# Key and value layers of a channel-mix block computed by Strassen's seven block products over 768 tokens

## The chip, the cores and the metric

The kernel runs on one core of one Trainium2 chip. The metric is the device time of one execution in microseconds (us); it is given as the median of several runs. TensorE (PE) does the matmuls, VectorE (DVE), ScalarE (ACT) and GpSimd (POOL) the element work, SyncE (SP) issues most transfers.

## The reference

Attention over 4 batches, 8 heads, 576 positions of 64 features (a coarse part over means of 4 positions plus a local band), then a normalised two-layer block with a residual (512 to 2048 to 512), then the channel-mix block that is changed here:

```python
xk = mu_k * x + (1.0 - mu_k) * x_prev      # x_prev: the token before
xr = mu_r * x + (1.0 - mu_r) * x_prev
k = np.maximum(xk @ w_k, 0.0)              # 512 -> 1024
v = k * k @ w_v                            # 1024 -> 512
r = 1.0 / (1.0 + np.exp(-(xr @ w_r)))      # 512 -> 512
return (r * v).astype(np.float32)
```

## The kernel before

Features lie on the 128 partitions, tokens on the free axis; the 2304 tokens are six chunks of N = 384. Every product of two float32 matrices is made from three matmuls in the reduced format fp32r (mm3, L203): high part times high part, high times low, low times high. For that each operand is split into a rounded copy (ACT) and the rest (DVE subtraction).

The first stage (the loop over c, to about 525 us) computes attention for chunk c + 1 beside the two-layer block of chunk c. slot(c) is called between groups of 12 matmuls, 56 times in each chunk, and lets one step of side work be issued each time: attention, the decoding of the next weights (the inputs are 64-bit floats, read as integers and converted by two ACT and two DVE operations of 128x512, decode, L75), and from chunk 1 on pre_b (L167), which loads, decodes and stores the weights of the last block to DRAM (bd), one step every third slot. In chunk 5, start_b and load_b bring these weights back and split them; emit_x2 writes the block's result x2d to DRAM, four 128x384 rows a chunk: DVE multiplies, POOL adds, POOL issues the stores. Attention's sums over four positions (sums, L241) are chains of adding transfers that POOL issues, each waiting for the one before.

The second stage (the loop over c from L827 on) goes through the six chunks: 8 groups of 12 matmuls for the key layer, 4 groups of 12 for the receptance and 4 groups of 24 for the value layer, 240 matmuls of 384 columns. Key results are evicted by ACT (relu), squared by DVE and split (ACT, DVE) into k2; the receptance takes a DVE clamp, ACT exp, a DVE addition and a DVE reciprocal; a value result is multiplied on DVE into ot and stored. mix(c, which) prepares xk and xr of the next chunk in the background. Matmul results lie in the eight banks of PSUM, used in turn (bank, L814).

The order of instructions on an engine is made by a scheduler that moves an instruction ahead where its inputs are ready sooner; in_order pins an instruction behind what stands before it on its engine, behind does the same for a named pair. Each engine runs its own queue strictly in order.

## Time and profile before

| | before |
|---|---|
| median of 3 runs | 780.17 us (779.93 to 780.19) |
| span of the profiled execution, first to last instruction | 778.9 us |
| PE busy | 761.7 us, 98% |
| DVE, ACT, POOL busy | 516.8, 372.5, 113.6 us |

The profile lists one execution, with its span; the runs' times lie around it, 1.0 to 1.3 us above. Busy time is the time in which an engine had an instruction; a busy PE can still be made of matmuls with gaps inside, so the rate of matmuls is read from first and last start. In the tables of stages, (x) counts instructions started there and PEclk is the granted TensorE clock as a share of full speed.

### The profile page before, as it was taken

How to read it: one execution, taken by the hardware profiler on the slowest of the kernel's cores; microseconds unless marked ns; L12 is line 12 of the kernel's file. 1: busy time of each engine (PE TensorE's matmuls, PEld its weight loads, DVE VectorE, ACT ScalarE, POOL GpSimd, SP SyncE). 2: the span in 40 equal slices, each digit the busy share in tenths (PEclk: the TensorE clock that was granted, in tenths of full speed). 3: DMA queues.
4: the chain of work that ended last, by engine and by line, in shares of the span. 5: the costliest groups of instructions: out<-in, count | busy, mean ns of one | idle time of the engine just before them, and what ended most of it. 6: DMA issues, size and time to landing. Idle time of an engine off the chain costs nothing.

```text
span 778.9 us, 13826 instructions
## 1 busy us (share of the span) xinstructions
PE 761.7 (98%) x5474; PEld 738.4 (95%) x5474; DVE 516.8 (66%) x1018; ACT 372.5 (48%) x840; POOL 113.6 (15%) x148
## 2 busy tenths in 40 slices
PE   5899999999999999999999999999999999999998
PEld 4789898999999999999999999999999999999998
DVE  6879996866456556655664447428949595968664
ACT  4679986455344543554353336317344344535230
POOL 3333300410044404410300030002000000000000
PEclk9859999999999999999999999999999999999999
DMA  8998744344327642744142014302110102010101
GB/s 246 265 295 225 205 140 143 99 116 147 107 79 165 145 131 68 183 123 129 58 124 82 1 42 149 123 1 82 32 50 21 62 11 72 1 42 0 42 1 41
DMA packets 47393, 78.81 MB, mean 101 GB/s; under 512 B 5856, under 2 KB 32096, under 8 KB 47328
## 3 DMA queue, kind: packets, MB, share of 16 engines
q1 hardware_dynamic: 37152, 67.89, 28.0%
q0 software_dynamic: 10176, 10.04, 6.9%
q8 instruction: 43, 0.70, 0.4%
q14 instruction: 22, 0.18, 0.1%
HBM read 63.22 MB, written 14.68 MB: 100 GB/s over the span
## 4 chain that ended last, share of the span: by engine, by line
PE 84%; DVE 7%; ACT 5%; DMA 2%; issue 1%; SPq 0%; ACTq 0%; DVEq 0%
PE b_ps L205 11%; PE b_ps L204 11%; PE b_ps L206 11%; PE acc L204 8%; PE h_ps L204 8%; PE acc L205 7%; PE acc L206 7%; PE h_ps L206 7%; PE h_ps L205 7%; PE av L429 2%; DMA raw<-in_w 2%; PE sc L351 1%; PE scd L347 1%; DVE rm L85 1%; ACT rm L84 1%; ACT rm L80 1%
## 5 line engine op out<-in xcount | busy, mean ns | idle before, releaser
L625 DVE SCALAR_TENSOR_TENSOR hl<-h_ps,hh 128x384 fp32r<-128x384 f32 x96 | 53.1, 553 | 81.9 <-ACT hh L624 81.5
L624 ACT ACTIVATE hh<-h_ps 128x384 fp32r<-128x384 f32 x96 | 46.7, 486 | 97.5 <-PE h_ps L206 97.3
L645 POOL TENSOR_TENSOR x<-x2t,x 128x384 f32<-128x384 f32 x24 | 24.2, 1023 | 302.2 <-DVE x2t L644 302.0
L206 PE MATMUL b_ps<-k,wbl 128*128 128x384 f32 x192 | 64.1, 334 | 0.0
L204 PE MATMUL b_ps<-xk,wbh 128*128 128x384 f32 x192 | 64.1, 334 | 0.0
L205 PE MATMUL b_ps<-xk,wbh 128*128 128x384 f32 x192 | 64.1, 334 | 0.0
L206 PE MATMUL b_ps<-xk,wbl 128*128 128x384 f32 x192 | 64.1, 334 | 0.0
L204 PE MATMUL b_ps<-k,wbh 128*128 128x384 f32 x192 | 64.1, 334 | 0.0
L205 PE MATMUL b_ps<-k,wbh 128*128 128x384 f32 x192 | 64.1, 334 | 0.0
L855 DVE RECIPROCAL e<-e 128x384 f32<-128x384 f32 x24 | 61.0, 2544 | 0.1
L85 DVE SCALAR_TENSOR_TENSOR rm<-rm 128x512 uint32<-128x512 uint32 x52 | 35.6, 688 | 16.3 <-ACT rm L84 15.6
L772 ACT ACTIVATE mixa<-x2in,vec_t 128x384 f32<-128x384 f32 x48 | 28.4, 613 | 37.0 <-DVE xr L775 34.8
L404 ACT COPY PT<-T 32x192 f32<-32x192 f32 x96 | 33.5, 349 | 24.7 <-DVE T L400 23.6
L835 ACT ACTIVATE kr<-b_ps 128x384 f32<-128x384 f32 x48 | 23.5, 490 | 45.5 <-PE b_ps L206 45.4
L247 POOL DMA_DIRECT2D kd<-in_kr x36 | 35.5, 987 | 66.7 <-DMA kd<-in_kr 63.5
L836 DVE TENSOR_TENSOR kr<-kr,b_ps 128x384 f32<-128x384 f32 x48 | 26.5, 552 | 22.6 <-ACT kr L835 22.6
L84 ACT ACTIVATE rm<-raw 128x512 uint8<-128x512 uint8 x52 | 40.3, 785 | 2.2 <-DVE rm L81 1.5
L248 POOL DMA_DIRECT2D vd<-in_vr x36 | 39.3, 1091 | 13.3 <-DMA vd<-in_vr 13.0
L825 DVE TENSOR_TENSOR k<-kr,k 128x384 fp32r<-128x384 f32 x48 | 27.4, 572 | 20.3 <-ACT k L824 20.3
L361 ACT ACTIVATE Pd<-scd,mx 96x144 f32<-96x144 f32 x48 | 17.6, 370 | 40.8 <-DVE mx L358 39.9
L80 ACT ACTIVATE rm<-raw 128x512 f32<-128x512 f32 x52 | 34.4, 669 | 3.8 <-DMA raw<-in_w 3.4
L204 PEld LDWEIGHTS b_ps<-xk,wbh 128*128 128x128 f32 x192 | 36.0, 188 | 0.0
(165 smaller groups left out, 2317.7 us busy)
## 6 DMA issues: line engine op xcount, KB each, us to landing
raw<-in_w SPq DMA_DIRECT2D x32, 512.0 KB, 6.2
v<-in_vw SPq DMA_DIRECT2D x24, 256.0 KB, 3.5
bd<-rm SPq DMA_DIRECT2D x20, 256.0 KB, 2.0
wf<-bd SPq DMA_DIRECT2D x10, 512.0 KB, 4.8
q<-in_qw SPq DMA_DIRECT2D x24, 208.0 KB, 4.1
kz<-in_kw SPq DMA_DIRECT2D x48, 102.0 KB, 2.7
x2d<-x POOLq DMA_DIRECT2D x24, 192.0 KB, 2.2
out<-ot SPq DMA_DIRECT2D x24, 192.0 KB, 1.9
```

The lines of the kernel that those rows point to most:

```text
L80: in_order(pinned, nc.scalar.activation(ru.bitcast(F32), raw.rearrange("p (n t) -> p n t", t=2)[:, :, 1].bitcast(F32), AF.Copy, scale=2.0 ...
L84: in_order(pinned, nc.scalar.activation(low, top, AF.Copy, scale=1.0 / 32.0, bias=-31.0 / 64.0))
L85: in_order(pinned, nc.vector.scalar_tensor_tensor(ru, ru, 3, m, op0=ALU.logical_shift_left, op1=ALU.bitwise_or))
L204: nc.tensor.matmul(ps, wh, ah, start=first, stop=False)
L205: nc.tensor.matmul(ps, wh, al, start=False, stop=False)
L206: nc.tensor.matmul(ps, wl, ah, start=False, stop=last)
L247: in_order(r > 0, eng.dma_start(kd, kr[b, hp, r], **op))
L248: in_order(r > 0, eng.dma_start(vd, vr[b, hp, r], **op))
L404: nc.scalar.copy(PT[p, :, j, :], T[p, :, 0:24])
L624: nc.scalar.activation(hh, ps[:, 0:N], AF.Relu)
L625: last_hl[0] = nc.vector.scalar_tensor_tensor(hl, ps[:, 0:N], 0.0, hh.bitcast(F32), op0=ALU.max, op1=ALU.subtract)
L855: nc.vector.reciprocal(e, e)
```

## The change

The key and value layers are multiplied as 2x2 blocks over two chunks at once (768 tokens, three rounds s instead of six chunks) with seven block products in place of eight (products). Each product is itself the three matmuls of mm3. Sums of weight blocks are formed in the first stage (pre_b: piece and combined), split there and stored to DRAM, and come back ready for use (load_w). Sums of token blocks are formed by seven, on POOL for the key layer and for the value layer of rounds 1 and 2, on DVE for round 0. The last stage is cut in two: all rounds of key and receptance first, with squared keys (kd2) and receptances (rd) stored to DRAM, then all rounds of the value layer, which load them back. The square moves from DVE to POOL, the receptance is one ACT sigmoid. Results in PSUM are read in part before a bank is added to again (after). pre_b takes a step at every slot from chunk 1 to the end of chunk 5.

The diff, cut to its core (the lines that it removes stand in the functions above):

```diff
+    rctx = ExitStack()
+    stg = rctx.enter_context(tc.tile_pool(name="stg", bufs=1, side="right"))
+    xp = rctx.enter_context(tc.tile_pool(name="xp", bufs=2, side="right"))
+    hp_ = rctx.enter_context(tc.tile_pool(name="hring", bufs=HB, side="right"))
...
+    def halves(v, other, dst):
+        store = lambda hl, part: nc.sync.dma_start(dst(hl), part if len(dst(hl).shape) == 2 else part.rearrange("p (k f) -> p k f", k=2))
+        in_order(True, nc.scalar.copy(other.bitcast(F32R), v))
+        yield True
+        store(0, other)
+        in_order(True, nc.vector.tensor_tensor(v.bitcast(F32R), v, other, op=ALU.subtract))
+        yield True
+        store(1, v)
...
+    def piece(src, keep, dst, key=None):
+        t = stg.tile([128, 1024], I32, tag="stg", name="raw", bufs=RB)
+        rm = stg.tile([128, 2, 512], U32, tag="stg", name="rm", bufs=RB)
+        a, b = held(), held()
+        yield from behind_slot(a)
+        nc.sync.dma_start(t if len(src.shape) == 2 else t.rearrange("p (k f) -> p k f", k=2), src)
+        yield True
+        yield True
+        yield from behind_slot(b)
+        g = decode(t, True, rm)
+        w = next(g)
+        other = spare.pop()
+        yield True
+        next(g, None)
+        freed[a] = True
+        yield True
+        if keep is not None:
+            nc.sync.dma_start(keep, w)
+            ready.add(key)
+        if dst is not None:
+            yield from halves(w, other, dst)
+        freed[b] = True
+        yield True
+    def combined(needs, x, y, op, keep, dst, key):
+        t = stg.tile([128, 2, 512], F32, tag="stg", name="comb", bufs=RB)
+        a = held()
+        yield from behind_slot(a)
+        while not needs <= ready:
+            yield False
+        nc.sync.dma_start(t[:, 0], x)
+        nc.sync.dma_start(t[:, 1], y)
+        yield True
+        yield True
+        in_order(True, nc.gpsimd.tensor_tensor(t[:, 0], t[:, 0], t[:, 1], op=op))
+        yield True
+        if keep is not None:
+            nc.sync.dma_start(keep, t[:, 0])
+            ready.add(key)
+        yield from halves(t[:, 0], t[:, 1], dst)
+        freed[a] = True
+        yield True
 
...
+        def quarter(g, m, k):
+            if g < 2:
+                return wks[:, g + 2 * k, 1024 * m:1024 * m + 1024]
+            g -= 2
+            return wvs[:, 4 * k + 2 * g:4 * k + 2 * g + 2, 512 * m:512 * m + 512]
+        def first(g, n):
+            m, k = n // 2, n % 2
+            to = {0: 0, 1: 1, 3: 3}.get(n)
+            return lambda: piece(quarter(g, m, k), fq[:, g, n], None if to is None else (lambda hl: stored(g, to, hl)), ("q", g, n))
+        def second(g, n):
+            A11, A12, A21, A22 = (fq[:, g, i] for i in range(4))
+            x, y, op, keep, to, *needs = {
+                1: (A21, A22, ALU.add, fs[:, g, 0], 4, ("q", g, 2), ("q", g, 3)),
+                2: (fs[:, g, 0], A11, ALU.subtract, fs[:, g, 1], 5, ("s", g, 1), ("q", g, 0)),
+                3: (A11, A21, ALU.subtract, None, 6, ("q", g, 0), ("q", g, 2)),
+                4: (A12, fs[:, g, 1], ALU.subtract, None, 2, ("q", g, 1), ("s", g, 2)),
+            }[n]
+            return lambda: combined(set(needs), x, y, op, keep, lambda hl: stored(g, to, hl), ("s", g, n))
+        jobs = []
+        for g in range(4):
+            jobs += [first(g, 0), first(g, 1)] + ([second(g - 1, 2)] if g else [])
+            jobs += [first(g, 2), first(g, 3)] + ([second(g - 1, 4)] if g else []) + [second(g, 3), second(g, 1)]
+        rest = [(lambda k=k: piece(wrs[:, k, :], None, lambda hl: wrd[:, hl, k, :])) for k in range(4)]
+        jobs += rest[:2] + [second(3, 2)] + rest[2:] + [second(3, 4)]
+        running, todo = [], iter(jobs)
+        while True:
+            while len(running) < RB:
+                j = next(todo, None)
+                if j is None:
+                    break
+                running.append(j())
+            if not running:
+                return
+            for g in list(running):
+                r = next(g, None)
...
@@ emit_x2
-            nc.gpsimd.dma_start(x2d[:, o, N * c:N * c + N], x[:, o, :])
+            st = (nc.gpsimd if c < NCH - 1 else nc.sync).dma_start(x2d[:, o, N * c:N * c + N], x[:, o, :])
+        last_x2.append(st)
...
-        if 1 <= c < NCH - 1 and slots[c] % PRE == 0:
+        if 1 <= c and slots[c] % 3 < PRE:
             next(pre, None)
         if c == NCH - 1 and fd.over():
             if not late:
-                run_all(pre)
                 start_b()
...
+    def load_w(nm):
+        src, W = {"wk": (wkd, WK), "wv": (wvd, WV)}[nm]
+        for p in ORD:
+            W[p] = wpool.tile(list(src.shape[0:1]) + list(src.shape[2:]), F32R, tag="w", name=nm)
+            nc.sync.dma_start(W[p].bitcast(F32), src[:, p])
+            yield
...
+                ld = nc.sync.dma_start(t[:, :, i, 1:SEG + 1], x2d[:, :, n0:n0 + SEG])
+            if s == 1:
+                behind(ld, last_x2[-1])
+        x2in[s] = t
...
+    def mixed(s, which, k, a):
+        t = x2in[s]
+        a4 = a.rearrange("p (i n) -> p i n", i=4)
+        nc.scalar.activation(a4, t[:, k, :, 1:SEG + 1], AF.Copy, scale=vec_t[:, 1 + which, k:k + 1])
+        nc.vector.scalar_tensor_tensor(a4, t[:, k, :, 0:SEG], omu[:, which, k:k + 1], a4, op0=ALU.mult, op1=ALU.add)
+    def seven(B, T, split, eng=nc.gpsimd):
+        sub = lambda o, a, b: eng.tensor_tensor(o, a, b, op=ALU.subtract)
+        B11, B12, B21, B22 = B
+        T1, T2 = T
+        split(0, B11)
+        sub(T1, B12, B11)
+        yield
+        sub(T2, B22, T1)
+        yield
+        split(5, T2)
+        yield
+        sub(B12, B22, B12)
+        split(1, B21)
+        yield
+        split(6, B12)
+        yield
+        sub(T2, B21, T2)
+        split(4, T1)
+        yield
+        split(3, T2)
+        yield
+        split(2, B22)
...
+    def prep_xk(s):
+        ops = xk[s] = {}
+        mt = left[0].tile([128, KT, T2N], F32, tag="mt", name="mt")
+        T = [left[0].tile([128, 2, N], F32, tag=f"T{i}", name="T") for i in range(2)]
+        for k in (0, 2, 1, 3):
+            mixed(s, 0, k, mt[:, k, :])
             yield
+        def split(p, v):
+            t = ops[p] = wpool.tile([128, 2, 2, N], F32R, tag="w", name="xk")
+            nc.scalar.copy(t[:, 0], v)
+            nc.vector.tensor_tensor(t[:, 1], v, t[:, 0].bitcast(F32), op=ALU.subtract)
+        yield from seven([mt[:, 2 * i:2 * i + 2, N * j:N * j + N] for i in range(2) for j in range(2)], T, split)
+    def prep_xr(s):
+        h, l = (right[0].tile([128, KT, T2N], F32R, tag=f"xr{i}", name="xr") for i in range(2))
+        xr[s] = h, l
+        for k in range(KT):
+            a = right[0].tile([128, T2N], F32, tag="mixa", name="mixa", bufs=2)
+            mixed(s, 1, k, a)
+            yield
+            nc.scalar.copy(h[:, k, :], a)
+            nc.vector.tensor_tensor(l[:, k, :], a, h[:, k, :].bitcast(F32), op=ALU.subtract)
             yield
...
-    for g in late["parts"]:
+    for g in [pre] + late["parts"]:
+    rctx.close()
+    right.append(b2ctx.enter_context(tc.tile_pool(name="br", bufs=1, side="right", reuse_waits="tile")))
+    load_x2(1)
...
+    def products(W, X, nk, quarters, done, feed):
+        nq = len(quarters)
+        b = {x: [bank() for _ in range(nq)] for x in "ABE"}
+        p1, u2, u3 = {}, {}, {}
+        def plus(ps, u, nm):
+            t = small(nm)
+            nc.vector.tensor_tensor(t, ps[:, 0:N], u, op=ALU.add)
+            return t
+        def after(p, q):
+            if p == 0:
+                p1[q] = small("p1")
+                nc.scalar.copy(p1[q], b["A"][q][:, 0:N])
+            elif p == 5:
+                u2[q] = plus(b["B"][q], p1[q], "u2")
+            elif p == 1:
+                done(q, 0, 0, b["A"][q], None)
+            elif p == 6:
+                u3[q] = plus(b["B"][q], p1[q], "u3")
+            elif p == 4:
+                done(q, 1, 1, b["E"][q], u3.pop(q))
+            elif p == 3:
+                done(q, 1, 0, b["B"][q], p1.pop(q))
+            else:
+                done(q, 0, 1, b["E"][q], u2.pop(q))
+        for p, x, start in ((0, "A", True), (5, "B", True), (1, "A", False), (6, "B", False), (4, "E", True), (3, "B", False), (2, "E", False)):
+            w = W[p]
+            xh, xl = X[p]
+            for q, cols in enumerate(quarters):
+                ps = b[x][q][:, 0:N]
+                for k in range(nk):
+                    wh, wl = w[:, 0, k, cols], w[:, 1, k, cols]
+                    for i, (a, m) in enumerate(((wh, xh), (wh, xl), (wl, xh))):
+                        nc.tensor.matmul(ps, a, m[:, k, :], start=start and k + i == 0, stop=k == nk - 1 and i == 2, skip_group_check=True)
+                after(p, q)
+                feed()
...
+    def load_wr():
+        for hl in range(2):
+            wr_t.append(wpool.tile([128, KT, 512], F32R, tag="w", name="wr"))
+            behind(nc.sync.dma_start(wr_t[hl].bitcast(F32), wrd[:, hl]), last_x2[-1])
+            yield
+    def rest(n):
+        for _ in range(n):
+            yield
+    bg = [rest(HOLD), load_wr()]
...
+    def prep_v(s, tiles):
+        X = vk[s] = {}
+        Bt, T = tiles()
+        for i in range(2):
+            for j in range(2):
+                n0 = T2N * s + N * j
+                last_kin[:] = [nc.sync.dma_start(Bt[2 * i + j], kd2[:, 4 * i:4 * i + 4, n0:n0 + N])]
+        def split(p, v):
+            h, l = X[p] = [wpool.tile([128, 4, N], F32R, tag="w", name="ko") for _ in range(2)]
+            nc.scalar.copy(h, v)
+            nc.vector.tensor_tensor(l, v, h.bitcast(F32), op=ALU.subtract)
+        yield
+        yield from seven(Bt, T, split, nc.gpsimd if s else nc.vector)
...
+    for s in range(NSC):
+        ops = xk[s]
+        X = {p: (ops[p][:, 0], ops[p][:, 1]) for p in ORD}
+        bg.append(prep_xr(s))
+        if s + 1 < NSC:
+            bg.append(prep_xk(s + 1))
+        else:
+            bg.append(load_w("wv"))
+            bg.append(prep_v(0, from_phase_k))
+        for half in range(2):
+            def done(q, i, j, ps, u):
+                f = 4 * i + 2 * half + q
+                t = small("k", "k", KB)
+                if u is None:
+                    nc.scalar.activation(t, ps[:, 0:N], AF.Relu)
+                else:
+                    nc.vector.tensor_tensor(t, ps[:, 0:N], u, op=ALU.add)
+                    nc.scalar.activation(t, t, AF.Relu)
+                nc.gpsimd.tensor_tensor(t, t, t, op=ALU.mult)
+                n0 = T2N * s + N * j
+                nc.sync.dma_start(kd2[:, f, n0:n0 + N], t)
+            products(WK, X, 2, [slice(128 * (2 * half + q), 128 * (2 * half + q) + 128) for q in range(2)], done, feed)
+        if s + 2 < NSC:
+            load_x2(s + 2)
+        xh, xl = xr[s]
+        for j in range(2):
+            for o in range(KT):
+                ps = bank()
+                c = slice(128 * o, 128 * o + 128)
+                n = slice(N * j, N * j + N)
+                for k in range(KT):
+                    mm3(ps[:, 0:N], wr_t[0][:, k, c], wr_t[1][:, k, c], xh[:, k, n], xl[:, k, n], k == 0, k == KT - 1)
+                t = small("r")
+                nc.scalar.activation(t, ps[:, 0:N], AF.Sigmoid)
+                n0 = T2N * s + N * j
+                nc.sync.dma_start(rd[:, o, n0:n0 + N], t)
+                feed(2)
+        flush()
...
+    for s in range(NSC):
+        if s + 1 < NSC:
+            bg.append(prep_v(s + 1, in_phase_v))
+            feed()
+        def done(q, i, j, ps, u):
+            o = 2 * i + q
+            n0 = T2N * s + N * j
+            r = small("rin", "r", 6)
+            behind(nc.sync.dma_start(r, rd[:, o, n0:n0 + N]), last_kin[0])
+            if u is None:
+                nc.vector.tensor_tensor(r, ps[:, 0:N], r, op=ALU.mult)
+            else:
+                t = small("v")
+                nc.vector.tensor_tensor(t, ps[:, 0:N], u, op=ALU.add)
+                (nc.vector if s == NSC - 1 else nc.gpsimd).tensor_tensor(r, t, r, op=ALU.mult)
+            nc.sync.dma_start(out[128 * o:128 * o + 128, n0:n0 + N], r)
+        products(WV, vk[s], 4, [slice(128 * q, 128 * q + 128) for q in range(2)], done, feed)
+        flush()
+SB = 8
+KB = 5
+HOLD = 6
+NSC = NCH // 2
```

## Rows read from the trace of the kernel before

**Rows 1.** the page's busy time of each engine and the chain that ended last

```profile
...
PE 761.7 (98%) x5474; PEld 738.4 (95%) x5474; DVE 516.8 (66%) x1018; ACT 372.5 (48%) x840; POOL 113.6 (15%) x148
...
PE 84%; DVE 7%; ACT 5%; DMA 2%; issue 1%; SPq 0%; ACTq 0%; DVEq 0%
```

**Rows 2.** busy time by stage: us, busy (x) PE, PEld, DVE, ACT, POOL, PEclk, DMA share, GB/s

```profile
...
608.90:650.50 41.60, 41.60 (x242) 41.60 (x241) 31.34 (x48) 18.04 (x36) 0.00 (x0) 1.00 0.12 39
```

**Rows 3.** the matmuls of the second stage: ns min/median/max, first and last start

```profile
...
L204 PE MATMUL b_ps<-xk,wbh x192: 334/334/334, 525.8 to 749.9; 128*128 128x384 f32 x192
...
L206 PE MATMUL b_ps<-k,wbl x192: 334/334/338, 551.1 to 775.2; 128*128 128x384 f32 x192
```

**Rows 4.** groups by line and shape: out<-in, shapes, xcount | busy us, mean ns

```profile
...
L855 DVE RECIPROCAL e<-e 128x384 f32<-128x384 f32 x24 | 61.0, 2544 | 0.1
...
L772 ACT ACTIVATE mixa<-x2in,vec_t 128x384 f32<-128x384 f32 x48 | 28.4, 613 | 37.0 <-DVE xr L775 34.8 <-DVE xk L775 1.0 <-DMA x2in<-x2d 1.0
L777 DVE SCALAR_TENSOR_TENSOR mixa<-x2in,omu,mixa 128x384 f32<-128x384 f32 x48 | 27.9, 614 | 2.0 <-DMA wf<-bd 1.1 <-ACT mixa L772 0.8
...
L836 DVE TENSOR_TENSOR kr<-kr,b_ps 128x384 f32<-128x384 f32 x48 | 26.5, 552 | 22.6 <-ACT kr L835 22.6
...
L645 POOL TENSOR_TENSOR x<-x2t,x 128x384 f32<-128x384 f32 x24 | 24.2, 1023 | 302.2 <-DVE x2t L644 302.0
L835 ACT ACTIVATE kr<-b_ps 128x384 f32<-128x384 f32 x48 | 23.5, 490 | 45.5 <-PE b_ps L206 45.4
...
L91 DVE TENSOR_TENSOR wbl<-wf,wbh 128x512 fp32r<-128x512 f32 x20 | 12.6, 686 | 6.6 <-ACT wbh L88 6.6
L853 ACT ACTIVATE e<-e 128x384 f32<-128x384 f32 x24 | 12.5, 525 | 29.2 <-DVE e L852 29.2
...
L768 ACT CAST xk<-mixa 128x384 fp32r<-128x384 f32 x24 | 12.1, 508 | 0.0
...
L516 ACT ACTIVATE xc<-xc 128x768 f32<-128x768 f32 x12 | 10.1, 843 | 1.1 <-DVE al L510 1.0
...
L268 POOL TENSOR_TENSOR vr<-vr 72x512 f32<-72x512 f32 x4 | 5.1, 1267 | 25.4 <-DMA vr<-in_vr 25.4
...
L673 ACT ACT_TABLE_LOAD x1 | 1.3, 1283 | 0.7 <-PEq L936 0.7
```

**Rows 5.** one line of attention's norm, six times: ns min/median/max

```profile
...
L518 DVE TENSOR_TENSOR xc<-xc x6: 946/957/2368, 75.9 to 464.2; 128x768 f32<-128x768 f32 x6
```

**Rows 6.** timeline of DVE at three places: start, us, instruction

```profile
...
147.25 2.37 DVE L518 TENSOR_TENSOR xc<-xc 128x768 f32<-128x768 f32 x1
...
461.70 0.56 DVE L644 TENSOR_TENSOR x2t<-acc,y 128x384 f32<-128x384 f32 x1 [1.40 <-POOL x L645]
...
529.72 1.30 DVE L825 TENSOR_TENSOR k<-kr,k 128x384 fp32r<-128x384 f32 x1 [0.58 <-ACT k L824]
```

**Rows 7.** timeline of POOL at the same places

```profile
...
147.76 1.02 POOL L645 TENSOR_TENSOR x<-x2t,x 128x384 f32<-128x384 f32 x1
...
460.65 1.99 POOL L645 TENSOR_TENSOR x<-x2t,x 128x384 f32<-128x384 f32 x2
...
529.56 1.03 POOL L645 TENSOR_TENSOR x<-x2t,x 128x384 f32<-128x384 f32 x1
```

**Rows 8.** busy time by stage, in the first stage

```profile
...
40.00:60.00 20.00, 19.73 (x109) 16.51 (x109) 14.66 (x32) 15.03 (x33) 5.29 (x6) 0.62 0.99 289
...
147.00:525.60 378.60, 378.56 (x2961) 367.50 (x2961) 211.79 (x472) 164.05 (x400) 70.83 (x88) 1.00 0.38 106
...
225.00:302.00 77.00, 77.00 (x633) 74.24 (x632) 45.91 (x105) 36.05 (x89) 25.49 (x31) 1.00 0.53 129
```

**Rows 9.** waits of POOL from 147 to 525 us: total us, times, longest

```profile
...
POOL kd L247 <- DMA kd<-in_kr: 27.1, 15, 3.7
```

**Rows 10.** DMA issues: count, KB each, median us to landing

```profile
...
bd<-rm SPq DMA_DIRECT2D x20, 256.0 KB, 2.0
...
out<-ot SPq DMA_DIRECT2D x24, 192.0 KB, 1.9
```

More of the change, by code (lines that the diff above doesn't have):

```diff
@@ L180, in load_b @@
[L180 to L201 removed]
+    fq = dram.tile([128, 4, 4, 512], F32, name="fq")
@@ new lines, in tile_block, with held, behind_slot @@
+    freed, ready = [], set()
+    def held():
+        freed.append(False)
+        return len(freed) - 1
+    def behind_slot(n):
+        while n >= RB and not freed[n - RB]:
+            yield False
+    def piece(src, keep, dst, key=None):
+        t = stg.tile([128, 1024], I32, tag="stg", name="raw", bufs=RB)
+        rm = stg.tile([128, 2, 512], U32, tag="stg", name="rm", bufs=RB)
+        a, b = held(), held()
[18 more added lines that the diff above has]
+        yield True
@@ L744, in start_b @@
         actx.close()
-        late["bp"] = bp = ctx.enter_context(tc.tile_pool(name="bp", bufs=1))
-        xk.extend(bp.tile([128, KT, NB], F32R, name=f"xk{i}") for i in range(2))
-        late["parts"] = [load_b(), mix(0, 0)]
+        left.append(bctx.enter_context(tc.tile_pool(name="bl", bufs=1)))
+        late["parts"] = [load_w("wk"), prep_xk(0)]
         load_x2(0)
-    def load_x2(c, pinned=False):
-        t = late["bp"].tile([128, KT, 2, SEG + 1], F32, tag="x2in", name="x2in", bufs=2)
-        for i in range(2):
-            n0 = NB * c + SEG * i
+    def load_w(nm):
[4 more added lines that the diff above has]
+            yield
@@ L755, in load_x2 @@
+    def load_x2(s):
+        t = (left if s % 2 == 0 else right)[-1].tile([128, KT, 4, SEG + 1], F32, tag="x2in", name="x2in")
+        for i in range(4):
+            n0 = T2N * s + SEG * i
             if n0 % S:
-                in_order(pinned, nc.sync.dma_start(t[:, :, i, :], x2d[:, :, n0 - 1:n0 + SEG]))
+                ld = nc.sync.dma_start(t[:, :, i, :], x2d[:, :, n0 - 1:n0 + SEG])
             else:
                 nc.gpsimd.memset(t[:, :, i, 0:1], 0.0)
-                in_order(pinned, nc.sync.dma_start(t[:, :, i, 1:SEG + 1], x2d[:, :, n0:n0 + SEG]))
@@ new lines, in small @@
+    def small(nm, tag="s", bufs=None):
+        return (right if tag == "k" else left)[-1].tile([128, N], F32, tag=tag, name=nm, bufs=bufs or SB)
+    def products(W, X, nk, quarters, done, feed):
[33 more added lines that the diff above has]
+                feed()
@@ new lines, in tile_block, with feed @@
+    kd2 = dram.tile([128, NK, B * S], F32, name="kd2")
+    rd = dram.tile([128, KT, B * S], F32, name="rd")
+    wr_t = []
+    def load_wr():
[5 more added lines that the diff above has]
+        for _ in range(n):
+            yield
+    bg = [rest(HOLD), load_wr()]
+    def feed(n=1):
+        for _ in range(n):
+            if bg and next(bg[0], 1) == 1:
+                bg.pop(0)
@@ new lines, in part, with from_phase_k @@
+    def part(t):
+        t = t.rearrange("p a b -> p (a b)") if len(t.shape) == 3 else t.rearrange("p a b c -> p (a b c)")
+        return [t[:, 4 * N * i:4 * N * i + 4 * N].rearrange("p (k n) -> p k n", k=4) for i in range(2)]
+    def from_phase_k():
+        mt = left[0].tile([128, KT, T2N], F32, tag="mt", name="kin")
+        a = right[0].tile([128, KT, 4, SEG + 1], F32, tag="x2in", name="kin")
+        b = left[0].tile([128, KT, 4, SEG + 1], F32, tag="x2in", name="kt")
+        return part(mt) + part(a), part(b)
@@ new lines, in tile_block, with in_phase_v @@
+    b2ctx.close()
+    bctx.close()
+    left.append(ctx.enter_context(tc.tile_pool(name="cl", bufs=1, reuse_waits="tile")))
+    right.append(ctx.enter_context(tc.tile_pool(name="cr", bufs=1, side="right", reuse_waits="tile")))
+    def in_phase_v():
+        T = part(right[-1].tile([128, KT, 4, SEG + 1], F32, tag="x2in", name="kt"))
+        return [right[-1].tile([128, 4, N], F32, tag="kin", name="kin", bufs=4) for _ in range(4)], T
+    for s in range(NSC):
+        if s + 1 < NSC:
+            bg.append(prep_v(s + 1, in_phase_v))
+            feed()
+        def done(q, i, j, ps, u):
[12 more added lines that the diff above has]
+        flush()
```

140 lines of the change are left out of this document (27 added, 113 removed).

## The prediction

> **What bounds the kernel now.** I began with the page: PE is busy 98% of the span, and the chain that ended last is PE for 84%; DVE's 7% and ACT's 5% are small beside it [rows 1]. They come early: from 147 to 525.6 us PE has work in 378.56 of 378.60 us [rows 8]. So where the change acts only two things can change the time: fewer matmuls, or a PE that waits. The stage table says how full the second stage is: in one chunk of 41.6 us PE has no gap, the granted clock is 1.00, and DVE (31.3), ACT (18.0) and POOL (0) have time to spare [rows 2]. First and last start of its matmuls are 525.8 and 775.2 us [rows 3]. A chunk holds 240 matmuls, so one costs 41.6 / 240 = 173.3 ns at 384 columns. That, and not the 334 ns that the rows give a single one (they overlap), is the price that I use. The other views price what the change puts on DVE, ACT and POOL: the groups by shape [rows 4], and a hunt for instructions that lasted longer than others of their line [rows 5 to 7].
>
> **Matmuls: minus 25.0 us.** Per round of two chunks the key layer had 2 x 96 matmuls and the value layer 2 x 96. Now each has 7 products x 8 pairs of 128-blocks x 3 = 168. Three rounds save 3 x 2 x 24 = 144; 144 x 173.3 ns = 25.0 us. Width, type and one weight load per matmul stay, so the price stays. The receptance keeps its 96 a round. What remains is 1296 x 173.3 ns = 224.6 us in place of 249.6.
>
> **Unit prices for the new element work.** DVE on 768 columns: 0.957 us [rows 5]; from 384 (0.552) that is 0.40 more, so the mixing operation of 0.614 becomes 1.02; with 686 ns at 512 columns the slope is 1.05 ns a column, 1.76 us at 1536. ACT: 0.49 to 0.53 at 384, 0.84 at 768, so mixing 0.95 and a split copy of 1536 columns 1.51. POOL: 1.02 at 384 and 1.27 at 512, 1.91 ns a column, so about 1.75 at 768 and 3.2 at 1536 [rows 4]. The sums for 768 and 1536 on POOL and for 1536 on DVE and ACT are estimates on these slopes.
>
> **A rule between DVE and POOL.** A 768-column subtraction or addition took 0.957 us in the median and 2.37 once; that one began at 147.25, and POOL added two SBUF tiles from 147.76 for 1.02. A 384-column split at 529.72 took 1.30 instead of 0.55 while POOL worked from 529.56 for 1.03. But a DVE operation with one input in PSUM ran inside a POOL pair (460.65 to 462.64) in its usual 0.56 [rows 4 to 7]. So a DVE operation on two SBUF tiles is held while POOL adds or multiplies, about as long as the POOL operation lasts. This matters because the change moves squares, block differences and the last products to POOL. The Trainium skill says the like (GPSIMD Engine Reference, Key points: POOL shares its SBUF interfaces with VectorE, in contention with instructions of two SBUF inputs), which the trace bears out; it gives no size. Without such holds the key terms below would be nothing and the time 760.
>
> **Key and receptance stage, per round: 168 + 96 matmuls, 29.1 + 16.6 us.** DVE reads PSUM 20 times (0.552 each, 11.0 us; not held), and does two-tile work of 8 mixings and 11 splits: 8 x 1.02 + 11 x 0.957 = 18.7 us. POOL does 16 squares and 4 differences, 16.4 + 7.0 = 23.4. ACT does 20 evictions, 8 mixings, 11 copies and 8 sigmoids: 31 us. In 45.7 us each fits alone. But 18.7 + 23.4 = 42.1 exclude each other, and most of it is issued in the key part of 29.1.
> PE feels it through the banks. A quarter of a product, six matmuls into one bank, takes 1.04 us, and a round has two halves of 14 quarters. At three products of a half PE adds again into a bank that DVE must have read (after), and comes back to it three quarters (3.1 us) after it was finished. The last such read of a round is the 16th of 20, due 27 quarters = 28.1 us after the start. What DVE must do by then:
> - Round 0: nothing in the background before the new right-hand space is free, when POOL's last row is done at 530.6, 4.8 us after the start [rows 3, 7]; less two reads, 3.7 us idle. Then 16 reads 8.8, four mixings and four splits of xr 7.9, four mixings of xk 4.1, and of ten squares begun by then three quarters in the way (DVE has two-tile work in 12 of 21 us, and a square that meets a read catches the operation behind it) 7.7, one difference 1.3. Sum 33.5: 5.4 us late.
> - Round 1: two xr and four xk mixings are left; the first two xr mixings have buffers of their own and can be done under the receptance. 8.8 + 5.9 + 4.1 + 7.7 + 2.6 = 29.1: 1.0 late.
> - Round 2: differences for the value layer are on DVE, three by then: 8.8 + 5.9 + 5.3 + 7.7 = 27.7: in time.
> Sum plus 6.4 us. Bounds: 0 if reads go ahead of background work, and 3 x (42.1 - 29.1) = 39 if all exclusive work must be done within the key part. I take the sum by due times, since the program issues the first reads of a half ahead of most of its background.
>
> **Value stage, per round 29.1 us.** In rounds 0 and 1, next operands: four POOL differences 12.9 and six products 6.1, seven DVE splits 12.3: 31.3 of exclusive work in 29.1, so up to 2.2 late a round, or 0 since a value product lasts 4.2 us and its reads are due 6.2 us later. Loads come in here: per round 3.1 MB of keys, 1.6 of receptances, and 7.3 MB of value weights, for which room is made only as the last key products end. By tile sizes the second stage moves 45 MB (squared keys out and in 18.8, receptances out and in 9.4, results 4.7, value and receptance weights 9.4, x2d 3.1) in 225 us, 200 GB/s, where 289 was the most the trace shows at a DMA share of 0.99 [rows 8], against 39 GB/s in a chunk before [rows 2]. I take 3 us for both rounds, bounds 0 and 8.
>
> **First stage.** 32 splits (DVE 0.69 each) and 16 POOL sums of 1.27 come in, and the 20 splits of load_b go: DVE plus 8 us net, plus up to 16 x 1.27 = 20 of holds, on 212 of 379 us; transfers of 256 KB rise from the equivalent of 40 to 120 and the key weights' 7.3 MB come in at its end, 28 MB more, which at 289 GB/s adds 0.26 to a DMA share of 0.38, or 0.2 to the 0.53 of the fullest stretch [rows 4, 8, 10]. Hidden by PE's 379 us of uninterrupted work; if the cover goes, ACT's copy behind a late POOL sum delays a relu and then PE. POOL waits for adding transfers 15 times, 27.1 us in all and 3.7 at the longest [rows 9]. ACT's copy is issued three slots behind its sum, some 4 us (225 to 302 us is one chunk of 56 slots [rows 8]), which covers such a wait; where a wait and the sum's own 1.27 come together I put 2 us, four times at the worst. I take 1 us, bounds 0 and 8.
>
> **Edits at nothing.** The DVE reciprocals (61 us) and the exp chain go, a sigmoid of about 0.53 comes, on engines off the path [rows 4]; one more table load of 1.28 lies under the receptance's matmuls. By the Trainium skill (ScalarE: Activation LUTs, What ACT_TABLE_LOAD costs) a switch costs 2.66 us with its drain; the trace shows only the 1.28, and either is hidden. The last x2d stores on SP, and the order of loads behind them, touch rounds 1 and later.
>
> **The end.** Behind the last matmul DVE now adds and multiplies, one operation of 0.55 more; the last store lands in 1.9 us as before [rows 4, 10]. Plus 0.6.
>
> **Sum.** 778.9 - 25.0 + 6.4 + 3 + 1 + 0.6 = 764.9 us span. The runs lie 1.3 above the span (780.17 against 778.9): **766.2 us**.
>
> **The rivals.**
> - *Clean*: every read is in time, no waits: 778.9 - 25.0 + 0.6 + 1.3 = 755.8. For it: DVE's 29.7 and ACT's 31 us are under 70% of a round's 45.7. Against it: the holds. Chance 0.24; with some of the waits gone it joins the forecast.
> - *First stage pays*: POOL sums behind adding transfers, or crowded DMA, hold ACT: forecast plus the other 7 to 8 = 774. Chance 0.10.
> - *Holds take the key part*: background work goes ahead of reads on DVE, each POOL operation is paid in full, PE stands in the key part of all rounds: 39 + 2 x 2.2 + 1 + 0.6 on 753.9 = 798.9 span, 800 us. It turns the sign once the three key parts lose more than 25.0 - 4.6 = 20.4 us, 6.8 each. For it: 42.1 us of exclusive work against 29.1. Against: a third of it can slip under the receptance. Chance 0.14; within 0.2% of before, its half-way house, 0.05.
> - That the saving is not made at all (matmuls dearer by the new layout) I leave out: operands and shapes are the same.
>
> **Numbers.** Forecast 0.47, with its own range 760 (no key term) to 771 (value term at its bound). What a measurement can tell here is about 0.2%, 778.6 to 781.7. Faster 0.24 + 0.47 + 0.10 = 0.81, same 0.05, slower 0.14. The range for 8 in 10 runs from the clean case to just under no change: 755.5 to 778.5.
>
> **What would show it.** Right: 1296 matmuls at 173 ns in the second stage; DVE splits and mixings of about twice their usual length beside POOL squares; waits of PE on DVE in the key part, longest in round 0, none in the receptance. Wrong: a PE without waits there (clean), PE waits before 525 us (first stage), PE waits of over 7 us in every round (slower), or PE waiting on a transfer in the value stage, which I price at 3 us at most for its likely case.

## The result: 787.8 us, slower by 1.1%

The changed kernel takes 787.78 us (median of 4 runs, 787.44 to 790.0) against 780.10 before: a ratio of 1.0109 (95%: 1.0088 to 1.013). The profiled execution took 787.44, its span 785.7, so 6.8 us more span than [rows 1]'s execution, where 14 less were forecast. The page of after, its busy line and the head of the chain that ended last:

```profile
PE 752.0 (96%) x5330; PEld 722.2 (92%) x5330; DVE 523.5 (67%) x926; ACT 389.3 (50%) x805; POOL 269.9 (34%) x240
...
PE 61%; DMA 14%; issue 12%; DVE 5%; POOL 4%; ACT 2%; SPq 1%; DVEq 0%; POOLq 0%; ACTq 0%
```

DMA, 2% of the chain before [rows 1], is 14% of it. The starts of the first and last product matmul place the loss:

| stretch | before | after | difference | forecast |
|---|---|---|---|---|
| first stage, until the first second-stage matmul | 525.8 | 542.1 | +16.3 | +1 |
| second stage, first to last start, matmuls alone | 249.4 | 224.5 | -25.0 | -25.0 |
| its waits: key part of round 0 | 0 | 5.3 | +5.3 | +5.4 |
| key parts of rounds 1 and 2 | 0 | 0 | 0 | +1.0 |
| receptance, 288 matmuls at 176 ns | 0 | 0.8 | +0.8 | 0 |
| value part | 0 | 8.3 | +8.3 | +3 |
| last start to end of span | 3.7 | 4.7 | +1.0 | +0.6 |

The 25 us are all there: 1296 matmuls, product matmuls at 173.3 ns. The first stage, which I costed at 1 us, takes two thirds of them back. What PE waited for in its uninterrupted stretch [rows 8] (us, times, longest):

```profile
PE acc L293 <- DVE hl L713: 4.0, 4, 1.4
PE mean L574 <- DVE sum_l L570: 2.6, 1, 2.6
PE av L517 <- ACT PdT L507: 0.8, 1, 0.8
PE scd L435 <- DVE x L535: 0.4, 1, 0.4
PE tp L504 <- DVE xc L624: 0.4, 1, 0.4
```

Seven of these eight waits are for DVE. The four for `hl` and the one for `sum_l` make 6.6 of the 8.2 us, and the timeline says what DVE was late with. One of the four waits for `hl`, first SP's queue and then DVE (start, length, what ended the idle time ahead):

```profile
253.75 0.32 SPq L231 DMA_DIRECT2D comb<-fq  x1
254.12 0.42 SPq L232 DMA_DIRECT2D comb<-fs  x1
254.63 0.38 SPq L321 DMA_DIRECT2D v<-in_vw  x1
255.11 0.38 SPq L312 DMA_DIRECT2D q<-in_qw  x1
...
260.01 0.55 DVE L365 TENSOR_REDUCE qdz<-q 64x96 f32<-64x384 f32 x1 [4.07 <-DMA q<-in_qw]
...
261.52 0.56 DVE L713 SCALAR_TENSOR_TENSOR hl<-h_ps,hh 128x384 fp32r<-128x384 f32 x1
262.13 0.19 PEld L293 LDWEIGHTS acc<-hl,w_1h 128*128 128x128 f32 x1 [1.44 <-DVE hl L713]
```

SP waited 2.9 us for a store before it could issue the first load for a weight sum at 253.75; the query load stands behind in the same queue and goes out at 255.11. DVE takes its work in order: it stands 4.07 us before the reduction of `q`, and `hl`, for which PE waits, is behind. Three of the four waits (1.2 to 1.4 us each) come behind such a load; the fourth is 0.2 us. Over the stage, from the query tile's view, after and then before:

```profile
  DMA q<-in_qw: 20.2, 9
...
DMA to landing us min/median/max: 2.7/3.9/5.4
```

```profile
  DMA q<-in_qw: 2.8, 5
...
DMA to landing us min/median/max: 2.6/3.8/4.7
```

From issue to landing a query load takes what it took before. These transfers are not slower; their issue is late. SP's own waits show the same. Before, the query loads stood at SP's head until the matmuls that still read their buffer were done; in the change the buffer is mostly free when SP gets to them (before, then after: us, times, longest):

```profile
SPq L224 <- PE sc L351: 46.5, 14, 16.4
...
SPq L312 <- PE sc L439: 3.7, 6, 1.1
```

The fifth wait:

```profile
302.47 0.69 DVE L187 TENSOR_TENSOR rm<-rm 128x512 fp32r<-128x512 f32 x1 [4.27 <-DMA fq<-rm]
303.08 0.55 DVE L570 TENSOR_TENSOR sum_l<-xsum,sum_h 128x384 fp32r<-128x384 f32 x1
...
303.69 0.19 PEld L574 LDWEIGHTS mean<-sum_l,ones_r 128*128 128x128 f32 x1 [2.94 <-DVE sum_l L570]
```

`halves` writes the low half over the piece (L187) while the store `fq<-rm` still reads it: 4.27 us, and PE waits: its weight load 2.9 us, the matmul itself 2.6. Behind it PE runs at half clock for ten matmuls, and after the longest wait of the value part for twenty (windows; PEclk is the granted clock, 0.50 being 1.2 GHz):

```profile
304.90:308.00 3.10, 3.10 (x11) 3.10 (x10) 1.22 (x3) 0.00 (x0) 0.00 (x0) 0.50 0.47 158
759.90:763.00 3.10, 3.10 (x11) 3.10 (x10) 3.10 (x3) 0.81 (x1) 3.10 (x2) 0.50 0.46 156
```

At 320 ns in place of 173 these cost 1.5 and 2.9 us. The last part of the loss has no wait at all: in the first stage the distance from one matmul's start to the next is 175.9 ns, 173.7 before. In five chunks of 384 layer matmuls that makes 5 x 384 x 2.2 ns = 4.2 us. With the 8.2 us of the waits above and 1.5 of slow clock that is 13.9 of the 16.3; the rest lies in pieces too small for these views.

The second stage: the three key parts and the value part's last stretch (us, then busy time of PE, PEld, DVE, ACT, POOL, granted clock, DMA share, GB/s):

```profile
542.07:576.52 34.45, 30.25 (x169) 28.97 (x169) 29.21 (x35) 22.61 (x35) 23.77 (x20) 1.00 0.73 233
593.42:622.54 29.12, 29.12 (x169) 29.12 (x169) 22.89 (x32) 19.99 (x33) 18.58 (x16) 1.00 0.40 135
639.44:668.56 29.12, 29.12 (x169) 29.12 (x169) 20.06 (x26) 13.03 (x24) 15.98 (x13) 1.00 0.44 163
...
740.00:781.00 41.00, 37.49 (x199) 36.63 (x197) 29.51 (x29) 9.40 (x8) 24.13 (x10) 0.92 0.42 140
```

Round 0's longest wait, 3.0 us, in the timeline:

```profile
568.92 2.55 POOL L869 TENSOR_TENSOR T<-mt,T 128x768 f32<-128x768 f32 x1
571.50 0.83 ACT L902 CAST xk<-T 128x768 fp32r<-128x768 f32 x1 [5.80 <-POOL T L869]
572.21 1.81 POOL L869 TENSOR_TENSOR mt<-mt 128x768 f32<-128x768 f32 x1
572.37 2.47 DVE L903 TENSOR_TENSOR xk<-T,xk 128x768 fp32r<-128x768 f32 x1 [1.66 <-ACT xk L902]
574.76 0.54 DVE L1069 TENSOR_TENSOR k<-b_ps,u 128x384 f32<-128x384 f32 x1
575.36 0.19 PEld L995 LDWEIGHTS b_ps<-xk,wk 128*128 128x128 f32 x1 [3.03 <-DVE k L1069]
```

A POOL difference makes ACT late, ACT makes a DVE split late, the split is held by the next POOL difference (2.47 in place of 0.96), and the PSUM read that PE needs is behind. The value part's longest, 3.85 us from one matmul's start to the next, has the same members:

```profile
752.82 3.54 POOL L869 TENSOR_TENSOR kt<-kin,kt 128x1536 f32<-128x1536 f32 x1
752.85 5.13 DVE L1037 TENSOR_TENSOR ko<-kin,ko 128x1536 fp32r<-128x1536 f32 x1
756.32 4.99 POOL L1116 TENSOR_TENSOR rin<-v,rin 128x384 f32<-128x384 f32 x2
758.86 0.48 ACT L973 COPY p<-b_ps 128x384 f32<-128x384 f32 x1 [0.99 <-POOL rin L1116]
759.40 1.01 PE L995 MATMUL b_ps<-ko,wv 128*128 128x384 f32 x2 [3.51 <-ACT p L973]
```

POOL's products stand behind its difference and last 2.5 us each; the copy waits for one of them, which gives back its buffer.

### The profile page after: what moved, and what is told of

Read it like the earlier page. It is cut to its first block, busy times and chain, and to the rows that moved or that the text cites. A ratio compares the mean times of both kernels' runs of the same rounds, so it can differ in the third digit from the quotient of the medians.

```text
span 785.7 us, 14146 instructions
## 1 busy us (share of the span) xinstructions
PE 752.0 (96%) x5330; PEld 722.2 (92%) x5330; DVE 523.5 (67%) x926; ACT 389.3 (50%) x805; POOL 269.9 (34%) x240
## 4 chain that ended last, share of the span: by engine, by line
PE 61%; DMA 14%; issue 12%; DVE 5%; POOL 4%; ACT 2%; SPq 1%; DVEq 0%; POOLq 0%; ACTq 0%
PE b_ps L995 17%; PE acc L292 5%; PE acc L293 5%; PE h_ps L292 5%; DMA kd<-in_kr 5%; PE acc L294 5%; PE h_ps L293 5%; PE h_ps L294 5%; PE b_ps L292 2%; PE b_ps L294 2%; PE b_ps L293 2%; DMA q<-in_qw 2%; PE av L517 1%; PE scd L435 1%; DMA vd<-in_vr 1%
## 5 line engine op out<-in xcount | busy, mean ns | idle before, releaser
L995 PE MATMUL b_ps<-ko,wv 128*128 128x384 f32 x504 | 92.3, 343 | 3.9 <-ACT p L973 3.5
L995 PEld LDWEIGHTS b_ps<-ko,wv 128*128 128x128 f32 x504 | 89.8, 193 | 5.7 <-ACT p L973 4.1
L995 PE MATMUL b_ps<-xk,wk 128*128 128x384 f32 x504 | 89.0, 335 | 4.2 <-DVE k L1069 2.7
L995 PEld LDWEIGHTS b_ps<-xk,wk 128*128 128x128 f32 x504 | 87.3, 188 | 5.5 <-DVE k L1069 3.0
L1071 POOL TENSOR_TENSOR k<-k 128x384 f32<-128x384 f32 x48 | 58.4, 1236 | 61.9 <-ACT k L1070 32.8
L1037 DVE TENSOR_TENSOR ko<-kin,ko 128x1536 fp32r<-128x1536 f32 x12 | 33.2, 2772 | 14.7 <-ACT ko L1036 10.7
L293 PE MATMUL acc<-hl,w_0h 128*128 128x384 f32 x96 | 32.8, 341 | 1.4 <-DVE hl L713 1.4
L293 PE MATMUL acc<-hl,w_2h 128*128 128x384 f32 x96 | 32.6, 339 | 1.4 <-DVE hl L713 1.4
L292 PE MATMUL h_ps<-ah,w_2h 128*128 128x384 f32 x96 | 33.8, 352 | 0.0
L293 PE MATMUL acc<-hl,w_1h 128*128 128x384 f32 x96 | 32.5, 339 | 1.2 <-DVE hl L713 1.2
```

The costliest lines, as they stand in the source:

```text
L292: nc.tensor.matmul(ps, wh, ah, start=first, stop=False)
L293: nc.tensor.matmul(ps, wh, al, start=False, stop=False)
L995: nc.tensor.matmul(ps, a, m[:, k, :], start=start and k + i == 0, stop=k == nk - 1 and i == 2, skip_group_check=True)
L1071: nc.gpsimd.tensor_tensor(t, t, t, op=ALU.mult)
```

## Experiments

**The place of the moving tiles.** In the changed kernel the first stage's moving tiles lie in the right-hand space. Reckoned from the tile sizes they start 480 bytes past a multiple of 512, where the weights, and before the moving tiles too, start at 96. No trace shows an address; what the runs show is what the shifts do.

a1, on the kernel before:

```diff
+    padp = ctx.enter_context(tc.tile_pool(name="padp", bufs=1))
+    pad = padp.tile([128, 96], F32, name="pad")
+    nc.gpsimd.memset(pad, 0.0)
     stg = ctx.enter_context(tc.tile_pool(name="stg", bufs=1))
```

> The kernel before, with 384 unused bytes per partition in front of the moving tiles of the first stage and of the key layer, so that these lie as far from a multiple of 512 bytes as the right-hand tiles of the changed kernel do (480 in place of 96). Theory 'place': the position of the moving tile costs about 2.3 ns a matmul (175 in place of 173 in the changed kernel's first stage); 2304 first-stage and 576 key matmuls make 6.6 us, so 786 to 787 us, with receptance and value matmuls still at 173. Rival 'traffic': the two nanoseconds come from the DMA traffic or from the high addresses, and 780.1 us stays.

786.54 us, ratio 1.0089 (1.0074 to 1.0104): 384 unused bytes cost 6.6 us, as expected. The groups of the second stage show which matmuls (xcount, busy us, mean ns): those whose moving tile moved, the key layer's, and not the value layer's.

```profile
L207 PE MATMUL b_ps<-xk,wbh 128*128 128x384 f32 x192 | 64.9, 338 | 0.0
...
L207 PE MATMUL b_ps<-k,wbh 128*128 128x384 f32 x192 | 64.2, 334 | 0.0
```

a2, the same three lines with `side="right"` on the changed kernel:

> The changed kernel, with 384 unused bytes at the top of the right-hand space, so that the moving tiles there lie 96 bytes past a multiple of 512, as the left-hand ones do. Theory 'place': 2304 first-stage and 288 receptance matmuls fall from 175 to 173 ns, 6.0 us less, about 782 us. Rival 'traffic' (DMA traffic or high addresses): 787.8 us stays.

784.83 us, but the five runs spread from 779.6 to 786.5, and the profiled one is the fastest of them; there the wait at 300 us was missing as well, while PE still waited 4.0 us for `hl`. The distances went back to 173.5 to 173.8 ns in first stage and receptance. The median is only 3.0 us under the change where 6.0 were expected: the distances are shown, their full worth in the changed kernel's time is not.

e1 to e3 are a1 with 32, 64 and 128 columns in `pad`; in e4 the pool of 96 columns stands ahead of the weights' pool:

> The kernel before with the same tiles shifted by 128 bytes in place of 384 (224 bytes past a multiple of 512, where 96 cost nothing and 480 cost 2.3 ns a matmul). Theory 'residue': how far the moving tile lies from a multiple of 512 decides, and 224 lies between; 173 ns if only a place near the end of the 512 costs, 174 to 175 if each place away from 96 does. Rival 'any shift': 175 ns and 786 us whatever the shift.

> The same with 256 bytes (352 past a multiple of 512). Theory 'residue': 173 if only the end of the 512 costs, more if not. Rival 'any shift': 175 ns, 786 us.

> The same with 512 bytes: the residue is 96 again. Theory 'residue': 173 ns and 780 us as in the kernel before. Rival 'any shift, or the higher address': 175 ns, 786 us.

> The same with the 384 bytes in front of the weights, so that weights and moving tiles all lie at 480. Theory 'moving tile alone': 175 ns in the first stage and now in receptance and value layer too, whose moving tiles lie among the weights: 2304 + 1440 matmuls, 8.6 us more, 788.6 us. Rival 'relation of moving tile to weights': 173 ns, 780 us.

One run each (the kernel before beside them: 777.8); the mean distance of successive matmuls, worked out from the starts in each trace, says more than the single time:

| bytes before the moving tiles | moving less weights, mod 256 | first stage, ns | key layer | receptance, value | us |
|---|---|---|---|---|---|
| 0 (before) | 0 | 173.7 | 173.3 | 173.3 | 780.1 |
| 128 (e1) | 128 | 175.9 | 176.0 | 173.3 | 786.5 |
| 256 (e2) | 0 | 173.7 | 173.3 | 173.3 | 780.7 |
| 384 (a1) | 128 | 175.9 | 176.0 | 173.3 | 786.5 |
| 512 (e3) | 0 | 173.7 | 173.3 | 173.3 | 780.9 |
| 384, weights too (e4) | 0 | 173.7 | 173.3 | 173.3 | 781.5 |

My theory of a residue to 512 was half right: it is 256, and it counts between moving tile and weights, since e4, with everything at 480, is as fast as before. As causes, any shift, the height of the address, and traffic (39 GB/s in the second stage of before, [rows 2]) fall.

**Late loads and the overwrite.** a3:

```diff
+    pq = actx.enter_context(tc.tile_pool(name="pq", bufs=3))
...
+            i = units.index(nxt) + 1
+            if i < len(units) and units[i][0] > 0:
+                load_q(*units[i])
```

> The changed kernel, with three buffers for the query tile in place of two and its load issued one unit earlier. Theory 'queue': SP stands in waits for sums and halves of the weights, so the query loads behind are issued late, DVE waits for them at its head (20.2 us) and the subtraction that PE needs stands behind. Then DVE's wait falls under 5 us and four PE gaps of 4.9 us together go: about 783 us, less if the gap at 300.7 goes too. Rival 'crowded transfers' or 'POOL holds DVE': the gaps stay, 787.8 us.

780.93 us (1.0016, 0.9998 to 1.0035), 7 less than the change. DVE waits for no query load any more, though they take 4.3 us to land; PE's waits for `hl` fall to 0.2 us. The wait for `sum_l` with the slow clock behind it is missing here too, though DVE still waits for `fq<-rm` (2.4 us at the longest), so the 7 us are not the query loads' alone. One new wait of 2.3 us for `scd` came with the new order.

a4:

```diff
-        in_order(True, nc.vector.tensor_tensor(v.bitcast(F32R), v, other, op=ALU.subtract))
+        in_order(True, nc.vector.tensor_tensor(lo.bitcast(F32R), v, other, op=ALU.subtract))
...
-            yield from halves(w, other, dst)
+            yield from halves(w, other, dst, t[:, 0:512].bitcast(F32))
```

> The changed kernel, with the low half of a weight piece written into the tile that its raw data came in, not over the piece itself. Theory 'overwrite': DVE's subtraction waits for the store that still reads the piece (9.0 us in all, 4.3 at once at 298 to 302 us), and that wait is PE's gap of 2.95 us at 300.7 with ten matmuls at 320 ns behind it: gone, about 783.5 us. Rival: the raw tile is held longer, so loads come later and as much is lost elsewhere, 787.8 us.

779.49 us (0.9994, 0.998 to 1.0008), 8 less than the change where 4 were expected: the wait for `sum_l` and the slow clock are gone, and of four waits for `hl` two remain, 1.7 us, with DVE's wait for query loads as long as it was (20.1). That DVE, rid of the overwrite, has slack for the other two would explain it; no run tests this. The edit is in `piece` alone, and it holds the raw tile longer; the weight sums (`combined`) still overwrite.

c1, the three edits (a2, a3, a4) together:

> The changed kernel with the three edits together: moving tiles shifted by 384 bytes, query loads a unit earlier, low halves written elsewhere. Theory (place of the tiles plus DVE behind late loads and overwrites make the first stage's loss of 16.3 us): first product at 526 to 528 us in place of 542.1, second stage as it was, 787.8 - 15 = 773 us. Rival (part of the loss is holds of DVE by POOL's 16 sums or the extra work itself): 776 to 780.

775.26 us (0.9943, 0.9929 to 0.9958), first product at 528.9. All that PE waits for from 147 us to there:

```profile
PE scd L450 <- DVE x L550: 0.6, 2, 0.4
PE tp L519 <- ACT PT L507: 0.5, 1, 0.5
```

Of 16.3 us 13.2 are back. (One execution each; d4, whose first stage is that of before, reached its first product 1.4 us earlier than before did.) Alone the three edits gave 3.0, 6.9 and 8.3 us, 18 in all, and together 12.5: the wait for `sum_l` with its slow clock, 4.1 us, is missing in the trace of each, so the three can't be added. The 3.1 that stay are not taken apart further. POOL's 16 sums are in c1 as in the change, so in c1 they cost at most these 3.1.

**The key part.** Both on c1. c3:

```diff
-        yield from seven([...], T, split)
+        yield from seven([...], T, split, nc.vector)
```

> The first of the three, with the block differences of the key layer (768 columns) on DVE in place of POOL. Theory 'holds': the gap of 3.05 us in round 0 is a DVE split that lasts 2.47 us beside a POOL difference and waits before that for ACT behind another difference; it goes, 2 to 3 us less. Rival 'DVE has too much to do in round 0': 3.8 us more work there make the gaps larger by 1 to 4 us.

769.82 us (0.9874, 0.9859 to 0.9889), 5.4 less: key part of round 0 31.2 us in place of 35.7 in c1, 0.7 of which is slow clock behind the longest wait. More work on DVE, and DVE is less late; of the gaps 1.0 and 0.6 us stay.

c4 feeds the background at half pace in round 0 (a counter around `feed`, `HOLD = 2`):

> The first of the three, with the background work of round 0 fed at every second quarter of the key products, the rest under the receptance. Theory 'background goes ahead of reads': the 5.3 us that round 0's key part loses fall under 1.5, 4 us less. Rival: the background must be done somewhere, and PE waits as long at the start of the receptance or of round 1.

774.45 us (0.9934), the same four gaps to 0.2 us. It tells nothing: in its trace DVE and POOL do the same operations at the same distance from the stage's start, to 0.3 us, from 552 us on, presumably since the scheduler moves an instruction ahead where its inputs are ready.

d3 is d1 (below) with the squares on ACT:

```diff
-                nc.gpsimd.tensor_tensor(t, t, t, op=ALU.mult)
+                nc.scalar.activation(t, t, AF.Square)
```

> The kernel with all differences on DVE, and the squares of the key layer on ACT in place of POOL, so that POOL does nothing beside the key products. Theory 'holds': the 1.5 us that round 0's key part still loses go, and DVE's mixings and splits of 768 columns last 0.96 to 1.02 us there in place of 1.09 to 1.44: 1 to 1.5 us under the kernel with POOL's squares. Rival: ACT has 8 us more a round in the key part and is late with the copies that PE waits for; no gain, or 1 to 3 us slower.

765.51 us (0.9807, 0.9791 to 0.9823), the fastest kernel here. PE has no wait in any key part. DVE's splits, first the changed kernel's and then those of d3 (mean ns):

```profile
L915 DVE TENSOR_TENSOR xr<-mixa,xr 128x768 fp32r<-128x768 f32 x12 | 14.1, 1182 | 20.8 <-ACT xr L914 20.7
...
L903 DVE TENSOR_TENSOR xk<-T,xk 128x768 fp32r<-128x768 f32 x6 | 8.6, 1440 | 1.7 <-ACT xk L902 1.7
```

```profile
L930 DVE TENSOR_TENSOR xr<-mixa,xr 128x768 fp32r<-128x768 f32 x12 | 11.4, 952 | 17.5 <-ACT xr L929 17.5
...
L918 DVE TENSOR_TENSOR xk<-T,xk 128x768 fp32r<-128x768 f32 x7 | 6.6, 953 | 4.2 <-ACT xk L917 4.2
```

**The value part.** c2, on c1:

```diff
-                (nc.vector if s == NSC - 1 else nc.gpsimd).tensor_tensor(r, t, r, op=ALU.mult)
+                nc.vector.tensor_tensor(r, t, r, op=ALU.mult)
```

> The one before, with the last products of the value layer (L1116) on DVE in all rounds. Theory 'POOL queue and holds': POOL's products last 2.0 us beside DVE's splits, in place of 1.0, and the differences of the next round's operands stand behind them, so that ACT is late for a copy that PE needs (3.85 us and 20 matmuls at 320 ns at 755.6). Without them the value stage loses 2 us or less in place of 8.3: 6 us under the one before. Rival: DVE's 3.3 us more a round delay its PSUM reads by as much and nothing is gained.

775.83 us (0.9955): nothing. The gap of 3.8 us is gone and one of 6.6 has come at 713:

```profile
714.09 5.20 DVE L1131 TENSOR_TENSOR rin<-v,rin 128x384 f32<-128x384 f32 x4
714.25 3.69 POOL L884 TENSOR_TENSOR kt<-kin 128x1536 f32<-128x1536 f32 x1 [5.04 <-DVE ko L1052]
...
719.21 0.55 DVE L982 TENSOR_TENSOR u<-b_ps,p 128x384 f32<-128x384 f32 x1
```

The second of the four products begins 0.3 us after the POOL difference, lasts 3.80 us and ends 0.4 after it; the other three take 0.55 each. The PSUM read behind them is late. The wait was moved, not removed, and the value part loses more than in c1 (below); its profiled execution is no slower because it reached its first product at 526.6 us, 2.3 earlier.

d1, on c3, puts the value layer's differences on DVE (`seven(Bt, T, split, nc.vector)`):

> The kernel with the first stage mended and the key differences on DVE (769.8), and the value layer's block differences (1536 columns) on DVE as well. Theory 'POOL's differences': a POOL difference of 3.5 us holds a DVE split beside it (2.8 us in the mean, up to 5.1) and makes ACT's split copies wait, and with them the copy that PE needs at 738.5 us. On DVE a difference takes 1.75 us: the gap of 3.74 us and the 20 matmuls at 320 ns behind it go, about 763 us. Rival 'DVE has too much to do': 7 us more a round put its PSUM reads as late, 769 us or more.

767.86 us (0.9842, 0.9822 to 0.9862): 2 less than c3, not 7. The gap of 3.74 us is gone and a split takes 1.83 us in place of 2.8, but gaps of 2.9 and 1.5 us have come, now for DVE reading PSUM, and behind the first of them eleven matmuls run at half clock. Both theories hold in part; the intervals of c3 and d1 just meet.

d2 is d1 and c2 together:

> The same, and the last products of the value layer on DVE too, so that POOL does nothing in the value stage. Theory 'holds': DVE's splits last 1.75 us again; DVE's own work is then 29.2 us in a round of 29.1, so the time stays at that of the kernel with the differences alone on DVE, or 1 to 2 us above. If it is several us faster than that, POOL's products were still in the way; if several slower, DVE is the limit of the value stage.

769.60 us (0.9862, 0.9845 to 0.9879): splits are at 1.75 us, and PE waits five times in the value part, 6.1 us in all, 4.5 of them for DVE. So DVE is late with nothing on POOL too. The 1.7 us above d1 lie within the two intervals.

By its matmuls' starts the value part, which loses 8.3 us in the change, loses 8.4 in c1, 10.2 in c2, 8.1 in c3, 6.4 in d1, 8.3 in d2 and 6.2 in d3. No edit takes much more than a quarter of it away. Just before the longest gap of d1 and of d3 POOL waits 4.7 and 6.4 us for a receptance load, a rival that no run tests.

**The receptance alone.** d4, on the kernel before:

```diff
-            nc.vector.tensor_scalar(e, ps[:, 0:NB], -87.0, None, op0=ALU.max)
...
+            nc.scalar.activation(e, ps[:, 0:NB], AF.Sigmoid)
```

> The kernel before, with the receptance by one sigmoid on ACT in place of clamp, exponential, addition and reciprocal. It was costed at nothing, since PE has no gap in the second stage of the kernel before: 780 us, within 1. Rival: the sigmoid's table load stands in front of an eviction that PE waits for, 1 to 3 us slower.

780.36 against 780.40 us, 1.0002 (0.9992 to 1.0011).

## Why the prediction was wrong

- **Matmuls, -25.0:** right to the tenth. But "matmuls dearer by the new layout", which I left out because operands and shapes are the same, was true: 2.2 to 2.7 ns for each matmul whose moving tile went to the right-hand space, 4.2 us in the first stage and 0.8 in the receptance. The diff shows the move (`side="right"`); no row of before can price it.
- **First stage, +1: the step that failed.** It measured 16.3, which is 15.3 of the 20.8 us by which the span missed the forecast. I priced transfers by their volume, a DMA share of 0.38 plus 0.26, and named ACT behind a late POOL sum as the one danger. ACT was not it, nor the volume: a query load still lands in 3.9 us, 3.8 before. What I didn't follow is the order on two queues: SP, where the attention's loads now stand behind stores and loads that wait for sums, copies and earlier stores, and DVE, where those loads are consumed in order ahead of `hl`. The overwrite in `halves` can be read in the diff too. Together with the place of the tiles c1 gives 13.2 of the 16.3 back. "PE's 379 us of uninterrupted work" did not hide it: DVE's waits of 2.9 to 4.3 us for query loads left PE standing 1.2 to 1.4 us each. The place of the tiles is 4.2 us of the stage by the distances; how the rest divides between late loads and overwrite stays open, since the edits overlap.
- **Rival "First stage pays":** the first stage did pay, at twice this rival's upper bound, but not by its conditions: in the trace ACT waits for no POOL sum, and the query loads landed as fast as before. Issue order and DVE made it.
- **Key part, +6.4:** measured 5.3, all of it in round 0, as forecast (5.4; round 1 0 in place of 1.0). The mechanism, a DVE operation on two SBUF tiles held beside POOL, is shown by c3 and d3: without POOL the splits are at 0.95 us and PE does not wait there (d3). My split of the sum was off: of 7.7 for squares and 1.3 for a difference, c3 and d3 show the reverse, 4.5 for the differences (35.7 to 31.2, with the 0.7 of slow clock) and 2.1 for the squares (31.2 to 29.1 in d3). I had not seen the chain over ACT. That the total came within 0.1 us although its parts did not is luck.
- **Value part, +3:** measured 8.3, just over my bound. As forecast, PE waited for no transfer. The sizes were wrong: I took splits at 1.76, products at 1.02 and POOL's differences at 3.2, where they last 2.8 or 2.3, 2.0 and 3.9 beside each other, so that the operands of the last round were still being made in it. My list of PSUM reads that PE waits for had DVE's alone; PE's longest wait, 3.5 us, is for ACT's copy of the first product, late behind POOL. And 2.9 of the 8.3 is a granted clock of 0.50 behind that wait, a term that I had nowhere. The holds are shown operation by operation, but not as the cause of the sum: d2, with POOL idle in the value part, loses 8.3 us as well. What would remove it stays open.
- **End, +0.6:** 1.0. **Sigmoid, 0:** 0.0 (d4).
- **Forecast as a whole:** the saving and the key part's charge stand. d3 has no wait left in the key part and most of the first stage back, but still loses 6.2 us in the value part; that its span, 763.3 us, lies near the 764.9 forecast for the change is chance and confirms nothing.

## What to carry to other kernels

A load that an in-order engine consumes must not stand behind stores that wait for background work: list, for each queue that the change adds to, what waits there and who is behind it, before adding up bytes. An operation moved to POOL is not free for DVE: two DVE operands in SBUF beside POOL's work cost about POOL's whole time, so a difference of 1.75 us on DVE can be cheaper than one of 3.5 on POOL that holds DVE for as long (5.4 us gained here for the key layer's, 2.0, barely clear of noise, for the value layer's). And a pool moved to another side moves its tiles' starts: compare them with those of the weights.

## What was not expected of the hardware

- A matmul of 384 columns starts every 176.0 ns in place of 173.3 when its moving tile lies 128 bytes off the weights, modulo 256, and every 173.3 ns when it lies 0, 256 or 512 off (six kernels above). Other distances were not tried.
- The hold between DVE and POOL works both ways: POOL's 384-column product lasts 2.0 us beside DVE's splits, 1.02 alone [rows 4]; a DVE product lasts 3.80 us beside a POOL difference, 0.55 without (c2). The Trainium skill (Trainium Architecture — The Big Picture, What this means for kernel authors) calls the pair's shared port an exclusive lock and no split of bandwidth. The runs agree: the product began 0.3 us after the difference, which lasted 3.69, and ended 0.4 after it.
- The granted clock fell to 0.50 for ten matmuls after a wait of 2.95 us in the first stage and for twenty after one of 3.85 in the value part, and not after one of 3.05 in the key part. Behind that same wait (3.03 to 3.05 us) in a2, a3, a4, c1, c2 and c4 it fell too, for nine to eleven matmuls, so from one execution the cost of a wait of this length can't be told.
